# A feed-forward layer in groups of 256 tokens, with the last five groups' down projection as seven quarter products

## The chip, the cores and the metric

The kernel runs on one core of one Trainium2 chip. The metric is the device time of one execution in microseconds (us). Before the change three runs took 238.29, 239.14 and 239.62 us, with a median of 239.14.

The engines are TensorE (PE in the profile; its weight loads are PEld), VectorE (DVE), ScalarE (ACT), GpSimd (POOL) and SyncE (SP, which here only issues DMAs). Each engine works through its own instructions in order. SBUF is the on-chip memory, PSUM holds what TensorE writes.

## The reference, cut to what matters

```python
# attention: 4 batches, 8 heads, 768 positions, head dimension 64
scores = q @ k.T / 8 - slope[h] * dist        # kept: 8 global keys, 96 local keys
a = softmax(scores)
x = concat_heads(a @ v)                        # [4, 768, 512]
# token mixer of rank 32, then a feed-forward layer
u = x + (x.T @ U @ V).T
out = u + relu(u @ w_ch1) @ w_ch2              # w_ch1 512 x 2048, w_ch2 2048 x 512
```

The last line is what the change is about: an up projection (`u @ w_ch1`), a relu, a down projection (`@ w_ch2`) and the residual sum.

## The kernel before

**Attention.** The work goes pair by pair of heads: 4 batches x 4 pairs = 16 pairs, numbered i. The first four pairs (the first batch) run by themselves while the weights load. From then on, the loop over i (line 656) interleaves the attention of pair i with the mixer of pair i - 1 and with the feed-forward of earlier batches. One pass of the loop issues, for pair i, three blocks of scores (`st_S`, lines 333 and 340; VectorE adds the bias with L362, into `sp`), two exps on ACT (`st_E`, L374), and for pair i - 1 the products with v (`st_V`, lines 386 and 390, evacuated by VectorE at L395 and L409 and cast by POOL at L410) and the mixer: `st_M1` (L419, cast by VectorE at L423), `st_MT` (L436, cast at L437), `st_M3` twice (L473, added into x at L478), a POOL cast (L482) and a DMA transpose into `uT` (`st_X`, L462). The mixer's and the v products share one PSUM buffer, `ob`.

**Feed-forward before.** A batch's 768 tokens are two groups of 384. A group's up projection is 16 units, one for each 128 columns of w_ch1: four matmuls of 128x384 (L508) into a PSUM tile `hps` (three buffers of the tag `th`, shared with the transposes of q and k), then a relu on ACT into `htr` (L512). Its down projection is, for each of its three tiles of 128 tokens, four units of four matmuls of 128x512 (L528), accumulated in a PSUM tile `cps` (two buffers); after the fourth, VectorE adds x into `osb` (L534) and SP stores it. The very last tile is done as two halves of 16 matmuls of 128x256 (L546), each added and stored by itself (L551).

**What sets the order.** The order is written out by hand: between the pieces of attention stand calls `fill(n)`, each of which issues n units from two queues, `ups_q` and `downs_q`. `fill` mixes them four downs to three ups as far as both are there; a group's downs wait until all of its ups are issued, ups may run one group ahead, and no downs are issued before iteration 7 (`held`). A pass has 10 units in iterations 4 to 8 and 13 from 9 on. The groups of batch 0 are queued (`queue_ff`) before the loop, those of a later batch b when its last pair's mixer is done, in iteration 5 + 4b; what is left after iteration 17 is issued back to back.

**Weights.** w_ch1 comes as four DMAs of 512 columns each from POOL's queue (`load_w1`, L205), w_ch2 as four of 512 rows (`load_w2`, L208). Two ups are begun early (`begin_up`, L491), on the parts of `uT` that are ready.

Of the kernel before, what the change touches and what calls it, by code (L numbers as in the profile page):

```python
# [11 lines left out]
FP32 = mybir.dt.float32  # L12
FP16 = mybir.dt.float16
# [7 lines left out]
def kernel(  # L21
# [40 lines left out]
    NTG = GT // P  # L62

# [93 lines left out]
    reli = cst.tile([P, 256], I32, name="reli")  # L157
    nc.gpsimd.iota(reli, pattern=[[-1, 256]], base=0, channel_multiplier=1)
    ident = cst.tile([P, P], FP32, name="ident")
# [13 lines left out]
    relcat = cst.tile([P, 3, 256], FP32, name="relcat")  # L173
# [3 lines left out]
    def finish_table(t):  # L177
        nc.gpsimd.tensor_scalar_max(t[0:NG, 0, 0:P], relB[0:NG, 0:P], float(-NL))
        nc.gpsimd.memset(t[0:NG, :, P:], float(-NL))
# [8 lines left out]
    finish_table(rel16)  # L188
# [167 lines left out]
    relf = relcat.rearrange("p a c -> p (a c)")  # L356

    def s_dve(i, hi, got):
        sc, c0, tot, r0 = got
        if c0 == 0:  # L360
            sps[i, hi] = scp.tile([P, W], FP32, name=f"sp{hi}", tag=f"sp{hi}", bufs=1)
        nc.vector.scalar_tensor_tensor(  # L362
            out=sps[i, hi][:, c0:c0 + tot], in0=sc[:, 0:tot],
            scalar=qk_scale / slope[2 * (i % NP) + hi], in1=relf[:, r0:r0 + tot],
            op0=ALU.mult, op1=ALU.add,
        )
# [120 lines left out]
    def begin_up(jt, dcs, ps=None):  # L487
        if ps is not None:
            begun[jt] = [ps, 0]
        for dc in dcs:  # L490
            nc.tensor.matmul(  # L491
                begun[jt][0][:, 0:GT], w1_16[:, dc, jt * P:(jt + 1) * P], uTs[0][:, dc, 0:GT],
                start=(dc == 0), stop=False,
            )
        begun[jt][1] = dcs[-1] + 1

    def queue_ff(b, g):
        ts = slice(g * GT, (g + 1) * GT)
        uT, tmp16, x_sb = uTs[b], tmps[b], xs[b]
        cell = {}  # L500

        def mk_up(jt):
            def go():
                if jt == 0:
                    cell["htr"] = ffp.tile([P, NJC, GT], FP16, name="htr", tag="htr")
                hps, done = begun.pop(jt) if jt in begun else (ps_th("hps"), 0)
                for dc in range(done, NDC):
                    nc.tensor.matmul(  # L508
                        hps[:, 0:GT], w1_16[:, dc, jt * P:(jt + 1) * P], uT[:, dc, ts],
                        start=(dc == 0), stop=(dc == NDC - 1),  # L510
                    )
# [256 lines left out]
```

## Time and profile before

| | |
|---|---|
| median of three runs | 239.14 us |
| the profiled execution | 239.37 us, of which the span from first to last instruction is 237.6 |
| granted TensorE clock | 1.000 |
| HBM | 27.46 MB read, 6.29 MB written, 142 GB/s over the span |
| loads of q, k, v | 16 DMAs of 384 KB each, some 6 us to landing |
| loads of w_ch1 and w_ch2 | 8 DMAs of 512 KB, 10.8 us to landing |
| stores | 23 DMAs of 256 KB (2.3 us), 2 of 128 KB (1.7 us) |

In the lines that are shown below, a group of instructions has its line of kernel.py, the engine, the operation, the names written and read, the shapes and a count; then the busy time in us and the mean duration of one in ns; then the time that the engine stood idle just before them, and what ended it. A row of the timeline or of the chain has the start in us and the length in us; `x8` is eight instructions. A row of the stretches has the busy time of each engine with the count of its instructions. The strips of digits are the busy tenths in 40 slices of the span. Matmuls are pipelined, so the duration of one is longer than the spacing of a series.

### The profile page before, as it was taken

To read this page: it belongs to the slowest core of one execution; us is meant where nothing else is said; L and a number is where in the kernel's file an instruction comes from. 1 tells how busy PE (TensorE), PEld (TensorE's weight loads), DVE (VectorE), ACT (ScalarE), POOL (GpSimd) and SP (SyncE) were. 2 spreads that over 40 slices of the span, in tenths; PEclk is the share of its full clock that TensorE was granted. 3 is DMA by queue.
4 is the path that set the end of the run, shared out by engine and by line. 5 is a ranking of instruction groups with operands and counts; after the bars stand their busy time and mean duration, and the time that the engine had idled before them with its cause. 6 is when DMAs were issued, how large, how long until landed. Compare 5 with 4: busy or idle time off the path is not lost.

```text
span 237.6 us, 4921 instructions
## 1 busy us (share of the span) xinstructions
PE 226.9 (96%) x1964; PEld 126.3 (53%) x1964; DVE 124.8 (53%) x277; ACT 115.9 (49%) x200; POOL 79.7 (34%) x128
## 2 busy tenths in 40 slices
PE   7889959999999999999999999999999999999994
PEld 2446645656554445565555455565555555555553
DVE  3778857768686867574766675765433111011121
ACT  6767757886750403865544227474632244533200
POOL 7379937576361524242425151313111000000000
PEclk9999999999999999999999999999999999999999
DMA  6998999999989998896949581751212210011012
GB/s 197 294 287 239 261 241 229 259 229 175 223 177 227 222 233 197 214 194 157 241 127 234 168 231 36 205 25 39 75 50 46 77 47 30 14 44 47 14 75 88
DMA packets 86558, 36.61 MB, mean 154 GB/s; under 512 B 74152, under 2 KB 83592, under 8 KB 86536
## 3 DMA queue, kind: packets, MB, share of 16 engines
q1 hardware_dynamic: 81480, 32.01, 55.9%
q0 software_dynamic: 5056, 4.29, 11.3%
q8 instruction: 15, 0.25, 0.4%
q14 instruction: 7, 0.06, 0.1%
HBM read 27.46 MB, written 6.29 MB: 142 GB/s over the span
## 4 chain that ended last, share of the span: by engine, by line
PE 78%; DMA 7%; POOL 4%; ACT 4%; DVE 3%; issue 1%; SPq 1%; POOLq 0%
PE cps L528 34%; PE hps L508 31%; DMA w<-in_moe_w_ch_dram 4%; DMA kst<-in_k_dram 3%; PE sc L333 3%; ACT ep L374 2%; ACT htr L512 2%; PE ob L390 2%; PE cps L546 1%; PE ob L386 1%; PE sc L340 1%; POOL v L127 1%; PE sc L473 1%; POOL vA L272 1%; PE ob L419 1%
## 5 line engine op out<-in xcount | busy, mean ns | idle before, releaser
L512 ACT ACTIVATE htr<-hps 128x384 f16<-128x384 f32 x128 | 61.2, 492 | 84.1 <-PE hps L508 83.5
L508 PE MATMUL hps<-uT,w 128*128 128x384 f16 x506 | 97.6, 326 | 0.7 <-DVE uT L455 0.3
L528 PE MATMUL cps<-w,htr 128*128 128x512 f16 x368 | 91.3, 379 | 0.0
L508 PEld LDWEIGHTS <-w 128*128 128x128 f16 x506 | 45.5, 98 | 31.5 <-issue 0.7
L362 DVE SCALAR_TENSOR_TENSOR sp<-sc,relcat 128x512 f32<-128x512 f32 (+1 forms) x72 | 43.3, 641 | 23.7 <-PE sc L340 14.2
L528 PEld LDWEIGHTS <-htr 128*128 128x128 f16 x368 | 33.7, 98 | 32.2
L534 DVE TENSOR_TENSOR osb<-cps,x_sb 128x512 f32<-128x512 f32 x23 | 15.9, 690 | 49.7 <-PE cps L528 49.4
L374 ACT ACTIVATE ep<-sp 128x1408 f16<-128x1408 f32 x24 | 32.8, 1373 | 12.5 <-DVE sp L362 12.5
L410 POOL CAST x<-x_sb 128x384 f16<-128x384 f32 x30 | 15.4, 514 | 49.7 <-DVE x_sb L409 49.7
L482 POOL CAST x<-x_sb 128x768 f16<-128x768 f32 x12 | 10.0, 830 | 37.3 <-DVE x_sb L478 37.3
L333 PEld LDWEIGHTS <-kT 64*128 64x128 f16 x192 | 8.3, 93 | 16.9 <-issue 14.9
L409 DVE TENSOR_TENSOR x_sb<-ob,rcp 128x384 f32<-128x384 f32 x30 | 16.7, 557 | 1.0
L333 PE MATMUL sc<-qT,kT 64*128 64x128 f16 x192 | 16.7, 221 | 0.0
L390 PE MATMUL ob<-v,ep 128*128 128x65 f16 x192 | 16.0, 194 | 0.0
L390 PEld LDWEIGHTS <-ep 128*128 128x128 f16 x192 | 13.7, 98 | 3.0 <-issue 0.3
L340 PE MATMUL sc<-qT,kA 64*128 64x128 f16 x160 | 14.6, 217 | 0.7 <-DVE kA L264 0.3
L127 POOL CAST v<-vst 128x768 f16<-128x768 f32 x16 | 13.4, 840 | 4.0 <-DMA vst<-in_v_dram 4.0
L352 ACT ACTIVATE ep<-sc 128x512 f16<-128x512 f32 (+1 forms) x24 | 12.1, 559 | 5.3 <-PE sc L340 4.2
L386 PE MATMUL ob<-vA,ep 128*128 128x65 f16 x160 | 14.1, 194 | 0.2 <-DVE vA L285 0.2
L113 POOL CAST k<-kst 128x768 f16<-128x768 f32 x14 | 11.8, 845 | 1.4 <-ACT ep L352 1.0
L386 PEld LDWEIGHTS <-ep 128*128 128x128 f16 x160 | 11.0, 97 | 2.1
L113 POOL CAST q<-qst 128x768 f16<-128x768 f32 x13 | 10.9, 842 | 0.0
(85 smaller groups left out, 173.6 us busy)
## 6 DMA issues: line engine op xcount, KB each, us to landing
qst<-in_q_dram SPq DMA_DIRECT2D x16, 384.0 KB, 6.2
kst<-in_k_dram SPq DMA_DIRECT2D x16, 384.0 KB, 5.9
vst<-in_v_dram SPq DMA_DIRECT2D x16, 384.0 KB, 6.2
out_dram<-osb SPq DMA_DIRECT2D x23, 256.0 KB, 2.3
w<-in_moe_w_ch_dram POOLq DMA_DIRECT2D x8, 512.0 KB, 10.8
vA<-v SPq DMA_DIRECT2D x8, 152.3 KB, 3.5
out_dram<-osb SPq DMA_DIRECT2D x2, 128.0 KB, 1.7
uT<-x SPq DMA_TRANSPOSE x12, 4.5
```

Of the source, the lines that this page charges most:

```text
L113: turn_over(st16.rearrange("p n h d -> p h n d"), st)
L333: nc.tensor.matmul(scs[hi][:, o:o + P], kT[r, kb * P:(kb + 1) * P], qT[r, kb * P:(kb + 1) * P], start=(o == 0 and not on_pe), stop=(o + P ...
L340: nc.tensor.matmul(scs[hi][:, o + P:o + 2 * P], kA[r, kb], qT[r, (kb + 1) * P:(kb + 2) * P], start=False, stop=(o + 2 * P == tot),)
L362: nc.vector.scalar_tensor_tensor(out=sps[i, hi][:, c0:c0 + tot], in0=sc[:, 0:tot], scalar=qk_scale / slope[2 * (i % NP) + hi], in1=relf[:, ...
L374: nc.scalar.activation(ep, sps.pop((i, hi)), AF.Exp, scale=slope[2 * (i % NP) + hi])
L386: nc.tensor.matmul(ob[:, qi], ep[:, OF[qi - 1]:OF[qi - 1] + P], vA[:, qi - 1, hi], start=True, stop=False,)
L390: nc.tensor.matmul(ob[:, qi], ep[:, DG[qi]:DG[qi] + P], vt[:, qi, hi], start=(qi == 0), stop=True,)
L409: nc.vector.tensor_tensor(xo, ob[:, :, 0:D], rb, ALU.mult)
L508: nc.tensor.matmul(hps[:, 0:GT], w1_16[:, dc, jt * P:(jt + 1) * P], uT[:, dc, ts], start=(dc == 0), stop=(dc == NDC - 1),)
L512: nc.scalar.activation(cell["htr"][:, jt], hps[:, 0:GT], AF.Relu)
L528: nc.tensor.matmul(cps, htr[:, jc, t * P:(t + 1) * P], w2_16[:, jc], start=(b > 0 and jc == 0), stop=(jc == NJC - 1),)
L534: nc.vector.tensor_tensor(osb, cps, x_sb[:, n], ALU.add)
```

## The change

A batch becomes three groups of 256 tokens. An up unit now takes two column tiles of w_ch1 into the two halves of one `hps` tile: eight matmuls of 128x256 and one relu of 128x512; a group has eight such units. `htr` gets three buffers. `fill` alternates one down and one up, the passes have 8, 10 and 11 units, and ups may run one group ahead (two while downs are held). The results are added into x itself and stored from there; `osb` is gone.

The last five groups, `WG` (batch 2 groups 1 and 2, batch 3 groups 0 to 2), compute the down projection of a group, a product of 256 x 2048 by 2048 x 512, by quarters: with A cut into a11, a12, a21, a22 (two halves of tokens, two of the inner dimension) and B into b11 to b22, seven products of 128 x 1024 by 1024 x 256 (a Strassen scheme in Winograd's form) stand for eight. Each is a unit of eight matmuls of 128x256, and after each VectorE adds what the half bank holds by then into x. That needs sums of the quarters: of the weights once (t1 to t4; t3 is written over b12, the others into a tile with the tag of x_sb), and of each group's `htr` (s1 to s4). A sum is issued in two halves on VectorE, from a queue `jobs`: one after each unit, or at once where a product needs it. In a split group the ups are ordered so that the sums of the first half can be issued after four of the eight ups.

Beside that, three setup tiles move (`reli` and `ident` share a buffer of `ep0`, and `relcat` has 640 columns instead of 768, read by a broadcast in the second block of scores).

```diff
+    FT = 2 * P
+    NFG = S // FT
+    HJ = NJC // 2
+    HD = DM // 2
+    WG = ((2, 1), (2, 2), (3, 0), (3, 1), (3, 2))
...
+    def queue_sum(name, part, out_, a, b_, op):
+        def go():
+            nc.vector.tensor_tensor(out_, a, b_, op)
+            have.add((name, part))
+        jobs.append(go)
+
+    def need(*names):
+        while not all(n in have for n in names):
+            jobs.popleft()()
...
+        t = xp.tile([P, 3, HJ, HD], FP16, name="t16", tag="x_sb", bufs=3)
+        b11, b12, b21, b22 = quarters
+        tw.update(t1=t[:, 0], t2=t[:, 1], t3=b12, t4=t[:, 2])
+        for name, a, b_ in (("t1", b12, b11), ("t2", b22, tw["t1"]), ("t4", b21, tw["t2"])):
+            for k, js in enumerate((slice(0, HJ // 2), slice(HJ // 2, HJ))):
+                queue_sum(name, k, tw[name][:, js], a[:, js], b_[:, js], ALU.subtract)
...
+            for name, a, b_, op in (
+                ("s1", "a21", "a22", ALU.add), ("s2", "s1", "a11", ALU.subtract),
+                ("s4", "a12", "s2", ALU.subtract), ("s3", "a11", "a21", ALU.subtract),
+            ):
+                queue_sum((name, b, g), k, cell[name][:, js], cell[a][:, js], cell[b_][:, js], op)
...
-        def mk_up(jt):
+        def mk_up(at):
+            jp = at // 2 + (at % 2) * NJC // 4 if split else at
+
             def go():
...
-                hps, done = begun.pop(jt) if jt in begun else (ps_th("hps"), 0)
-                for dc in range(done, NDC):
-                    nc.tensor.matmul(
-                        hps[:, 0:GT], w1_16[:, dc, jt * P:(jt + 1) * P], uT[:, dc, ts],
-                        start=(dc == 0), stop=(dc == NDC - 1),
-                    )
-                nc.scalar.activation(cell["htr"][:, jt], hps[:, 0:GT], AF.Relu)
+                hps, done = begun.pop(jp) if jp in begun else (ps_th("hps"), 0)
+                for k in range(2):
+                    jt = 2 * jp + k
+                    for dc in range(done, NDC):
+                        nc.tensor.matmul(
+                            hps[:, k * FT:(k + 1) * FT],
+                            w1_16[:, dc, jt * P:(jt + 1) * P], uT[:, dc, ts],
+                            start=(dc == 0 and k == 0), stop=(dc == NDC - 1 and k == 1),
+                        )
+                nc.scalar.activation(
+                    cell["htr"][:, 2 * jp:2 * jp + 2].rearrange("p j t -> p (j t)"), hps, AF.Relu
+                )
+                if split and at % 4 == 3:
+                    queue_sums(at // 4)
             return go
...
-                    osb = ffp.tile([P, DM], FP32, name="osb", tag="osb", bufs=3)
-                    nc.vector.tensor_tensor(osb, cps, x_sb[:, n], ALU.add)
-                    nc.sync.dma_start(out[b, n * P:(n + 1) * P, :], osb)
+                    nc.vector.tensor_tensor(x_sb[:, n], cps, x_sb[:, n], ALU.add)
+                    store(n)
+                    if t == 1 and follow in WG:
+                        queue_last_weight_sum()
             return go
...
+        def mk_product(bank, half, a, w, dst, first=False, done=None):
             def go():
...
+                need(*(((a, b, g), k) for k in range(2) if a[0] == "s"))
+                need(*((w, k) for k in range(2) if w[0] == "t"))
+                ps = cell[bank][:, half]
+                for j in range(HJ):
+                    nc.tensor.matmul(
+                        ps, cell[a][:, j], tw[w][:, j], start=(first and j == 0),
+                        stop=(done is not None and j == HJ - 1), skip_group_check=True,
+                    )
+                n, cs = dst
+                nc.vector.tensor_tensor(x_sb[:, n, cs], ps, x_sb[:, n, cs], ALU.add)
+                for what in done or ():
+                    store(*what)
             return go
...
+            x1 = mk_product("cx", lo, "a11", "b11", (n0, lo), first=True)
+            x2 = mk_product("cx", lo, "s2", "t2", (n0, hi_))
+            x3 = mk_product("cx", lo, "s3", "t3", (n1, hi_), done=[(n1, hi_)] if last else None)
+            x4 = mk_product("cx", lo, "a22", "t4", (n1, lo), done=[(n1, lo)] if last else [(n1,)])
+            y1 = mk_product("cy", lo, "a12", "b21", (n0, lo), first=True)
+            y2 = mk_product("cy", hi_, "s1", "t1", (n1, hi_))
+            y3 = mk_product("cy", hi_, "s4", "b22", (n0, hi_), done=[(n0,)])
+            for made in (x1, y1, x2, y2, x3, y3, x4) if last else (x1, y1, y2, x2, y3, x3, x4):
+                downs_q.append((made, (b, g)))
...
     def fill(n):
         for _ in range(n):
...
+            unit()
+            if jobs:
+                jobs.popleft()()
+
+    def unit():
+        down = downs_q and not held[0] and not any(w == downs_q[0][1] for _, w in ups_q)
+        room = ups_q and (not downs_q or place(ups_q[0][1]) - place(downs_q[0][1])
+                          < (3 if held[0] else 2))
+        if down and (ahead[0] > 0 or not room):
+            ahead[0] = 0
+            downs_q.popleft()[0]()
+        elif room:
+            ahead[0] = 1
+            ups_q.popleft()[0]()
...
-        n = 1 if i < 2 * NP + 1 else 2
+        units = iter(
+            (1, 1, 1, 1, 1, 1, 1, 1, 0) if i + 1 < NPE
+            else (1, 1, 1, 2, 1, 1, 1, 1, 1) if i < 2 * NP + 1
+            else (2, 1, 1, 2, 1, 1, 1, 1, 1)
+        )
```

More of the change, by code (lines that the diff above doesn't have):

```diff
@@ L515, in mk_down @@
         def mk_down(t, part):
-            n = NTG * g + t
+            n = 2 * g + t
             def go():
+                if (t, part) == (0, 1) and not split and follow in WG:
+                    queue_weight_sums()
                 if part == 0:
@@ L696 @@
             break
-        more = 1 if i + 1 < NPE else 0
-        fill(n + more)
+        fill(next(units))
         if live:
@@ L712 @@
             st_E(i, 0)
-        fill(1)
+        fill(next(units))
         if i > NP:
@@ L728 @@
             turn(i + 2)
-        fill(n - more)
+        fill(next(units))
     while ups_q or downs_q:
```

150 lines of the change are left out of this document (78 added, 72 removed).

## The prediction

> **What bounds the kernel now.** I read the page's totals first, then the busy times by stretch, then the groups by shape, then the order of time on TensorE.
>
> ```profile
> span 237.6 us, 4921 instructions
> PE 226.9 (96%) x1964; PEld 126.3 (53%) x1964; DVE 124.8 (53%) x277; ACT 115.9 (49%) x200; POOL 79.7 (34%) x128
> PE   7889959999999999999999999999999999999994
> DVE  3778857768686867574766675765433111011121
> PE 78%; DMA 7%; POOL 4%; ACT 4%; DVE 3%; issue 1%; SPq 1%; POOLq 0%
> ```
>
> ```profile
> 40.00:50.00 10.00, 9.33 (x102) 5.64 (x100) 6.91 (x13) 8.00 (x15) 7.29 (x12) 1.00 1.19 250
> 50.00:140.00 90.00, 89.87 (x829) 49.31 (x826) 61.55 (x136) 42.27 (x64) 35.74 (x52) 1.00 0.94 200
> 150.00:160.00 10.00, 9.87 (x100) 6.11 (x97) 6.37 (x15) 7.16 (x13) 1.76 (x3) 1.00 0.69 116
> ```
>
> The columns of the stretches are length, then busy PE, weight loads, DVE, ACT, POOL, the granted clock (1.00 throughout) and DMA. From 50 us on TensorE has hardly an idle moment: what shortens its instruction stream there shortens the kernel, and what makes it wait lengthens it. Before 50 us it waits for other things, and a change there is worth what it does to those waits. VectorE has 36% to spare beside attention and almost everything after 172 us.
>
> **What the feed-forward costs on TensorE, before and after.**
>
> ```profile
> L508 PE MATMUL hps<-uT,w 128*128 128x384 f16 x506 | 97.6, 326 | 0.7 <-DVE uT L455 0.3
> L491 PE MATMUL hps<-uT,w 128*128 128x384 f16 x6 | 1.3, 328 | 2.0 <-DMA w<-in_moe_w_ch_dram 2.0
> L528 PE MATMUL cps<-w,htr 128*128 128x512 f16 x368 | 91.3, 379 | 0.0
> L546 PE MATMUL cps<-w,htr 128*128 128x256 f16 x32 | 3.7, 273 | 0.0
> L546 PEld LDWEIGHTS <-htr 128*128 128x128 f16 x32 | 3.1, 98 | 0.6
> ```
>
> ```profile
> 181.48 4.32 PE cps L528 x20
> 199.85 3.90 PE hps L508 x24
> ```
>
> ```profile
> 230.61 3.66 PE L546 MATMUL cps<-w,htr 128*128 128x256 f16 x32
> ```
>
> A duration (326, 379 ns) contains the way through the array; the spacing is what counts. The pieces of the chain give 4.32/20 = 216 ns for 512 columns and 3.90/24 = 162.5 ns for 384. The timeline's row for 256 columns gives (3.66 - 0.273)/31 = 109.3 ns, with a weight load of 98 ns still hidden under it. So the fixed part of a step is 2 to 3 ns, and a step costs by its columns.
>
> - Up projection: 506 + 6 = 512 steps x 162.5 ns = 83.2 us become 4 x 3 x 64 = 768 steps of 256 columns x 109.3 ns = 83.9 us: **+0.7 us**.
> - Down projection: 368 x 216 ns + 32 x 109.3 ns = 83.0 us become 224 x 216 ns (seven plain groups) + 5 x 7 x 8 = 280 steps x 109.3 ns (the split groups) = 79.0 us: **-4.0 us**. Each split group needs 56 x 109.3 ns = 6.1 us where 32 x 216 ns = 6.9 us stood.
>
> Together **-3.3 us**, all of it on the engine that sets the end. Everything below is subtracted from that.
>
> The Trainium skill ("TensorE: Matmul & The Clock Gate", section Back-to-back issue gap) gives a sustained spacing of about 81 ns at 128 columns and 131 ns at 512, by which narrow steps would be poor value. Here the spacings are 109.3 and 216 ns; by the Trainium skill, interpolated as an estimate, a product step would take 98 ns, a split group 5.5 us against 4.2 us, and the change would lose. The trace disagrees with these spacings of the Trainium skill.
>
> **The first ups, 34 to 50 us.** The built order of the changed kernel has the eight units of the first group in loop iteration 4, each unit taking two column tiles of w_ch1; so units 3, 5 and 7 are the first that need quarters 1, 2 and 3 of w_ch1. Before, iteration 4 issued ten units of one tile each, tiles 0 to 9, and quarter 3 was first needed behind the transposes at 43.95 us.
>
> ```profile
> L205 POOL DMA_DIRECT2D w<-in_moe_w_ch_dram x2: 742/746/750, 27.5 to 28.2; - x2
> DMA to landing us min/median/max: 11.6/12.9/14.2
> ```
>
> ```profile
> 34.11 0.48 PE L508 MATMUL hps<-uT,w 128*128 128x384 f16 x2 [0.32 <-DVE uT L455]
> 35.39 0.81 PE L508 MATMUL hps<-uT,w 128*128 128x384 f16 x4
> 36.54 2.12 PE L508 MATMUL hps<-uT,w 128*128 128x384 f16 x12
> 38.87 2.77 PE L508 MATMUL hps<-uT,w 128*128 128x384 f16 x16
> 41.58 0.23 PE L333 MATMUL sc<-qT,kT 64*128 64x128 f16 x2
> 43.95 0.49 PE L233 MATMUL tp<-ident,q 128*128 128x128 f16 x6 [0.23 <-ACT htr L512]
> ```
>
> ```profile
> 34.90 1.27 DVE L362 SCALAR_TENSOR_TENSOR sp<-sc,relcat 128x512 f32<-128x512 f32 x2
> ```
>
> ```profile
> PE ob L419 <- POOL x L410: 0.4, 1, 0.4
> ```
>
> Quarter 2 lands at 27.5 + 11.6 = 39.1 us, quarter 3 at 28.2 + 14.2 = 42.4 us (the minimum is the first load's); the change leaves these loads and what stands ahead of them on POOL alone. The working for the new order: the second block of scores still ends at 36.5 us, because it waits for the two adds that VectorE ends at 36.17. Units 3 and 4 take 2 x 0.87 us, to 38.3; the third block of scores to 38.7; then a wait of 0.45 us for quarter 2; units 5 and 6 to 40.9; a wait of 1.6 us for quarter 3; units 7 and 8 to 44.25. The scores of iteration 5 then start at 44.3 instead of 41.58, 2.7 us later. In that time 16 x 256 instead of 10 x 384 columns have been issued, two thirds of an old unit or 0.45 us more work: a loss of 2.2 us. Two waits of iteration 5 shrink as the other engines catch up meanwhile (the 0.23 us at 43.95 and the 0.4 us of L419 for POOL): 0.55 us back. **+1.65 us**. From 50 us on TensorE has no slack in which to make it up. The bounds are 1.0 (more is given back, or the loads land earlier) and 2.7 (nothing is).
>
> **The half sums, about 145 to 172 us.** The sums of the split groups are new VectorE work: eight of 128x1024 f16 for the weights, then eight of 128x512 f16 in each of five groups, and 35 adds of 128x256 in place of 10 of 128x512. For groups 2 to 5 of these (after 172 us) VectorE is a tenth busy, so they are hidden; what counts is the stretch in which the weight sums and the first group's sums meet the last two attention pairs. No row shows an f16 add with both inputs in SBUF. The nearest:
>
> ```profile
> L362 DVE SCALAR_TENSOR_TENSOR sp<-sc,relcat 128x512 f32<-128x512 f32 x48 | 31.1, 685 | 17.3 <-PE sc L340 14.2 <-ACT htr L512 2.3 <-ACT ep L374 0.8
> L534 DVE TENSOR_TENSOR osb<-cps,x_sb 128x512 f32<-128x512 f32 x23 | 15.9, 690 | 49.7 <-PE cps L528 49.4
> L551 DVE TENSOR_TENSOR osb<-cps,x_sb 128x256 f32<-128x256 f32 x2 | 0.8, 424 | 2.4 <-PE cps L546 2.4
> L308 DVE COPY kA<-kT 128x640 f16<-128x640 f16 x8 | 2.5, 316 | 0.0
> ```
>
> At one element a cycle a sum of 512 costs 690 ns and one of 1024 costs 690 + 512 x 266/256 = 1222 ns; at two, 424 and 690 ns. The f16 copy (640 elements in 316 ns) shows that f16 can go faster than one, so I take 424 and 690 ns; even the copy's rate would give no less than about 290 and 415 ns. Eight of each is 8.9 us. They are popped one per unit over some 17 us, in which VectorE has 3.6 us in 10 free, 6.2 us, and some 2 us more because queued operations overlap: two adds of 685 ns took 1.27 us above, 0.1 us less than their sum, and there are over twenty operations. That just about fits. Where it doesn't, the engine's queue is in order, so behind a sum stand the casts between the transposes of the mixer (M1, MT, M3), each with one unit of 0.87 us to spare on TensorE, and the single `ob` buffer. One such place can be read off the new order: the first sum of the second split group is issued in the same unit as the up whose relu it needs, so it holds VectorE until 0.8 us after that up; with its own 0.42 us, the cast behind it ends about 0.45 us after TensorE wants it.
>
> Beside a POOL cast this can be worse, as these two rows show, where a copy that takes 0.28 us by itself takes 0.96:
>
> ```profile
> 22.27 0.96 DVE L285 COPY vA<-v 8x520 f16<-8x520 f16 x1
> 27.49 0.28 DVE L285 COPY vA<-v 8x520 f16<-8x520 f16 x1
> ```
>
> ```profile
> 22.25 0.84 POOL L113 CAST q<-qst 128x768 f16<-128x768 f32 x1
> ```
>
> The Trainium skill ("SBUF — State Buffer", section Who interferes with whom) states for a VectorE operation with two SBUF inputs that it and a GpSimd operation that reads SBUF lock each other out. The trace has no such operation, only the copy above, which agrees in kind.
>
> Bounds for this stretch: 0 (all fits) and +4 (the sums at one element a cycle add 6.4 us more to a full VectorE, of which the later group's slack returns a third). I take **+0.8 us**, nearer to nothing since the two-element price is nearer to the f16 row: 0.45 for the place named and the rest for collisions with POOL.
>
> **The rest.** The last group's products alternate between two PSUM banks, so an add (0.42 us, and 273 - 109 ns for the last columns' way through the array) has 0.87 us; with sums queued ahead of it the first repeat is some 0.15 us late: **+0.15 us**. The end is unchanged in shape, a 256-wide add and a 128 KB store after the last matmul. Relus:
>
> ```profile
> L512 ACT ACTIVATE htr<-hps 128x384 f16<-128x384 f32 x128 | 61.2, 492 | 84.1 <-PE hps L508 83.5
> L352 ACT ACTIVATE ep<-sc 128x512 f16<-128x512 f32 x16 | 8.7, 594 | 4.3 <-PE sc L340 4.2
> ```
>
> ```profile
> 95.32 0.86 ACT htr L512 x2
> 96.18 1.27 ACT ep L374
> 97.88 1.46 PE hps L508 x8
> ```
>
> 96 x 0.594 = 57 us replace 61.2 us, so ACT is no bound. Three hps buffers now cover 2.6 us of TensorE instead of 1.95, more than an exp (1.37 us) and a relu; the chain passes through ACT at 95 to 97 us and the ups behind it take 1.46 instead of 1.30 us. Two such places should go: **-0.3 us**. Storing x_sb itself instead of osb changes no wait, since nothing writes these rows again; t16 reuses the buffer of batch 1, whose last store is issued some eight units before the first weight sum.
>
> **The sum.** -3.3 + 1.65 + 0.8 + 0.15 - 0.3 = -1.0 us. The profiled execution took 239.37 us (span 237.6 and 1.8 around it), 0.2 more than the median of the three runs, 239.14; the forecast for a run is 239.14 - 1.0 = **238.1 us**, with a range of its own of 236.9 to 239.3.
>
> **Rivals.**
> 1. *VectorE falls behind* in the stretch of the weight sums: at more than about 0.55 us for a 512-wide sum the work no longer fits, and the mixer's casts, then the scores' buffers, hold TensorE. The stretch costs 3.3 us instead of 0.8: 240.6 us, slower. For it: 64% busy before, in-order queue, POOL rows above. Against it: f16 copies at half the time per element.
> 2. *The early wait is given back or smaller, and the sums fit*: 1.0 instead of 1.65 and 0.1 instead of 0.8, and the removed waits are 0.6: 236.4 us. For it: queued VectorE operations overlap. Against it: quarter 3 lands at 42.4 us whatever TensorE does.
> 3. *Seven products don't run as seven*: each waits for the add before it on its half bank, 0.27 us at 15 places, 4 us, and the saving is gone: 242 us. Against it: an up stands between two products in four of the five groups.
> 4. *Narrow steps gain little*: if halving the columns took off a quarter and not half, a step of 256 would cost 0.75 x 216 = 162 ns, and the 280 product steps 14.8 us more: 253 us. The row of the 32 steps speaks against it. The spacings of the Trainium skill above would have this sign.
>
> **How the numbers follow.** 0.5% of 239.14 is 1.2 us, about what a measurement of this kernel can tell from no change. The forecast has 0.50 (0.20 of it beyond -1.2 us, 0.30 within), rival 2 has 0.24, rival 1 has 0.22, rival 3 has 0.03, rival 4 has 0.01. Faster by over 0.5%: 0.20 + 0.24 = 0.44; within: 0.30; slower: 0.26. The range goes from rival 2 with every uncertain cost at its low end (235.9) to rival 1 with the stretch at +4 (241.3).
>
> **What would show it.** On TensorE in the changed kernel: steps of 128x256 spaced 109 ns; two waits for w_ch1 near 39 and 41 to 42.4 us, 2.0 us together; no waits of ups for ACT in the dense stretches; in the stretch of the last two pairs, waits for VectorE casts of under 1 us in all, and f16 sums of 0.42 and 0.69 us. Wrong would be: sums of 0.7 and 1.2 us, w_ch1 landing before 41 us, or waits between a group's products.

## The result and the profile after

The changed kernel takes **236.8 us** (median of 8 runs, 236.26 to 237.52), the kernel before 239.47 on the same chip (8 runs, 238.18 to 240.74): a ratio of **0.9893, 95% interval 0.9861 to 0.9926**, which is 2.6 us less (1.8 to 3.3). Unedited copies gave 0.9906 [0.9871, 0.9940] for the changed kernel and 1.0001 [0.9976, 1.0026] for the kernel before. The forecast was 238.1 us: the sign and the full range (235.9 to 241.3) held, but the result lies just below the forecast's own range (236.9 to 239.3), and 1.0 us less had been expected where 2.6 came. The profiled execution took 236.67 us.

The totals of the changed kernel's page, with the strips of TensorE and VectorE:

```profile
span 234.8 us, 5675 instructions
PE 224.0 (95%) x2324; PEld 161.4 (69%) x2324; DVE 151.4 (65%) x349; ACT 112.2 (48%) x169; POOL 80.3 (34%) x128
PE   7989977999999999999999999999999999999994
DVE  3677866468686777566667576779896543454452
```

VectorE went from 124.8 to 151.4 us busy, and its strip shows where: a hill of 9, 8 and 9 in the slices from 158 to 176 us, which the strip of before did not have. The same kernel by stretches (length, then busy PE, weight loads, DVE, ACT, POOL, the granted clock, DMA):

```profile
40.00:50.00 10.00, 8.57 (x111) 6.99 (x111) 5.45 (x11) 7.04 (x10) 5.46 (x9) 1.00 1.20 252
50.00:140.00 90.00, 89.68 (x916) 58.19 (x915) 61.22 (x135) 41.87 (x53) 36.05 (x54) 1.00 0.90 195
160.00:165.00 5.00, 5.00 (x63) 3.37 (x60) 4.97 (x10) 1.52 (x3) 1.91 (x3) 1.00 0.35 92
170.00:175.00 5.00, 5.00 (x58) 4.46 (x56) 4.97 (x10) 2.52 (x5) 0.83 (x1) 1.00 0.17 58
```

TensorE lost time at 40 to 50 us (8.57 of 10 where before had 9.33), and nothing to speak of later, although VectorE is busy 4.97 us in 5 in two stretches. The groups by shape:

```profile
L582 PE MATMUL hps<-uT,w 128*128 128x256 f16 x756 | 96.4, 273 | 2.1 <-DMA w<-in_moe_w_ch_dram 1.7 <-DVE uT L464 0.3
L519 DVE TENSOR_TENSOR s<-htr 128x512 f16<-128x512 f16 x20 | 9.3, 463 | 12.7 <-ACT htr L587 12.7
L632 PE MATMUL cx<-t,s 128*128 128x256 f16 x40 | 5.2, 273 | 0.0
L519 DVE TENSOR_TENSOR s<-htr,s 128x512 f16<-128x512 f16 x10 | 4.2, 420 | 0.2
L519 DVE TENSOR_TENSOR t<-w,t 128x1024 f16<-128x1024 f16 x4 | 2.6, 682 | 0.0
```

Products (L632) wait for nothing, ups (L582) wait 1.7 us for w_ch1, and the f16 sums take 420 and 682 ns (424 and 690 were assumed), except two, of 0.98 and 0.72 us, that stretch the mean of the row `s<-htr` to 463. Their cause is looked for below.

**One number apart from the medians.** The first up can start when the first quarter of w_ch1 has landed, and that moment turned out to vary from execution to execution. These are TensorE's first early up in the timeline of before, and in that of the changed kernel, and, of the changed kernel, the first product of the mixer (L428) for the last time but two, and the last product of all (start, length):

```profile
31.65 0.50 PE L491 MATMUL hps<-uT,w 128*128 128x384 f16 x2 [2.01 <-DMA w<-in_moe_w_ch_dram]
```

```profile
30.43 0.61 PE L502 MATMUL hps<-uT,w 128*128 128x256 f16 x4 [0.78 <-DMA w<-in_moe_w_ch_dram]
...
155.76 0.30 PE L428 MATMUL ob<-u,x 128*128 128x32 f16 x6
...
230.44 1.04 PE L632 MATMUL cx<-t,htr 128*128 128x256 f16 x8
```

From the start of the first up to the end of the last matmul is 234.27 - 31.65 = 202.62 us before (the last row of before, 230.61 + 3.66, stands in the prediction) and 231.48 - 30.43 = 201.05 us after: **1.57 us less**. This stretch hardly depends on when the quarter landed: two executions of the reordered kernel below, whose first ups start 2.03 us apart, agree in it to 0.01 us. So it tells a part of the change to some tenths, where a median of six runs tells 0.8 us. But loads that land later than the first quarter can still add to it: the 0.23 us between the two executions of the changed kernel are nearly all the wait for quarter 2.

A still shorter stretch is sharper: from the L428 row above (155.76 us in the changed kernel, just ahead of its first weight sum; L419 in the kernel before) to the end of the last matmul. Executions of one kernel agree in it to 0.02 us. It can be compared only between kernels that issue the same work ahead of that row, so among the rows of before, or among the others, and not across. The table has both stretches for every kernel; the ratio is to the kernel before on the same chip. A run that is over 1.5% longer than the fastest of its kernel is left out of the ratio, which concerns one run of before and one of the weight sums twice (245.30 us, the profiled one).

| kernel | median us (runs) | ratio, 95% interval | first up at | first up to last matmul | L428 to last matmul |
|---|---|---|---|---|---|
| before, first profile | 239.14 (3) | | 31.65 | 202.62 | 80.93 |
| before, copy | 239.17 (12) | 1.0001 [0.9976, 1.0026] | 31.57 | 202.60 | 80.93 |
| before, setup tiles moved | 238.66 (12) | 1.0008 [0.9983, 1.0034] | 30.93 | 203.06 | 80.93 |
| changed | 236.80 (8) | 0.9893 [0.9861, 0.9926] | 30.43 | 201.05 | 75.72 |
| changed, copy | 236.18 (6) | 0.9906 [0.9871, 0.9940] | 29.83 | 200.82 | 75.70 |
| groups of 256 alone | 240.42 (7) | 1.0067 [1.0043, 1.0092] | 30.92 | 204.10 | 79.02 |
| sums left out | 235.98 (6) | 0.9875 [0.9839, 0.9910] | 30.55 | 200.50 | 75.05 |
| first ups reordered | 236.09 (6) | 0.9887 [0.9839, 0.9934] | 31.51 | 199.51 | 75.71 |
| the same again | 235.09 (6) | 0.9856 [0.9815, 0.9897] | 29.48 | 199.50 | 75.70 |
| sums ahead of the unit | 236.58 (11) | 0.9915 [0.9885, 0.9945] | 30.55 | 200.92 | 75.87 |
| reordered and sums ahead | 236.17 (6) | 0.9892 [0.9856, 0.9927] | 31.64 | 199.68 | 75.87 |
| weight sums twice | 243.58 (6) | 1.0185 [1.0144, 1.0227] | 32.91 | 207.31 | 81.95 |
| all sums twice | 250.34 (6) | 1.0497 [1.0466, 1.0528] | 30.67 | 214.40 | 89.41 |
| weight sums on GpSimd | 240.33 (10) | 1.0087 [1.0053, 1.0121] | 28.89 | 206.32 | 80.57 |

Two executions of one kernel agree in the first of the two stretches to 0.23 us or better, while their first up starts up to 2 us apart. Between kernels it can differ by more without a cause in the edit: with the setup tiles moved it is 0.44 us longer, all of it one wait for a GpSimd cast at 68.6 us, and the second stretch is the same.

### The profile page after: what moved, and what is told of

The parts are those of the page before. It is cut to its first block, busy times and chain, and to the rows that moved or that the text cites. A ratio compares the mean times of both kernels' runs of the same rounds, so it can differ in the third digit from the quotient of the medians.

```text
span 234.8 us, 5675 instructions
## 1 busy us (share of the span) xinstructions
PE 224.0 (95%) x2324; PEld 161.4 (69%) x2324; DVE 151.4 (65%) x349; ACT 112.2 (48%) x169; POOL 80.3 (34%) x128
## 4 chain that ended last, share of the span: by engine, by line
PE 77%; POOL 7%; DMA 7%; DVE 3%; ACT 1%; issue 1%; SPq 0%; POOLq 0%
PE hps L582 32%; PE cps L612 21%; PE cx L632 7%; DMA w<-in_moe_w_ch_dram 6%; PE cy L632 5%; PE sc L339 3%; PE ob L399 2%; DMA kst<-in_k_dram 2%; PE ob L395 1%; POOL v L132 1%; POOL x L419 1%; PE sc L346 1%; POOL vA L278 1%; PE tp L239 1%; POOL k L118 1%
## 5 line engine op out<-in xcount | busy, mean ns | idle before, releaser
L587 ACT ACTIVATE htr<-hps 128x512 f16<-128x512 f32 x96 | 56.9, 597 | 87.2 <-PE hps L582 84.4
L582 PE MATMUL hps<-uT,w 128*128 128x256 f16 x756 | 96.4, 273 | 2.1 <-DMA w<-in_moe_w_ch_dram 1.7
L582 PEld LDWEIGHTS <-w 128*128 128x128 f16 x756 | 70.3, 98 | 13.2 <-DMA w<-in_moe_w_ch_dram 2.2
L612 PE MATMUL cps<-w,htr 128*128 128x512 f16 x224 | 56.9, 379 | 0.0
L612 PEld LDWEIGHTS <-htr 128*128 128x128 f16 x224 | 19.1, 97 | 16.6
L419 POOL CAST x<-x_sb 128x384 f16<-128x384 f32 x30 | 15.8, 526 | 42.2 <-DVE x_sb L418 38.8
L519 DVE TENSOR_TENSOR s<-htr 128x512 f16<-128x512 f16 x20 | 9.3, 463 | 12.7 <-ACT htr L587 12.7
L418 DVE TENSOR_TENSOR x_sb<-ob,rcp 128x384 f32<-128x384 f32 x30 | 16.7, 557 | 1.0
L632 PEld LDWEIGHTS <-s 128*128 128x128 f16 x160 | 15.5, 98 | 1.9
L399 PEld LDWEIGHTS <-ep 128*128 128x128 f16 x192 | 13.7, 98 | 2.6 <-DVE x_sb L418 0.3
L637 DVE TENSOR_TENSOR x_sb<-cx,x_sb 128x256 f32<-128x256 f32 x20 | 8.5, 423 | 10.1 <-PE cx L632 10.0
L632 PEld LDWEIGHTS <-htr 128*128 128x128 f16 x120 | 11.7, 98 | 1.3
```

Source lines behind the costliest of these rows:

```text
L399: nc.tensor.matmul(ob[:, qi], ep[:, DG[qi]:DG[qi] + P], vt[:, qi, hi], start=(qi == 0), stop=True,)
L418: nc.vector.tensor_tensor(xo, ob[:, :, 0:D], rb, ALU.mult)
L419: nc.gpsimd.tensor_copy(x16, xo)
L582: nc.tensor.matmul(hps[:, k * FT:(k + 1) * FT], w1_16[:, dc, jt * P:(jt + 1) * P], uT[:, dc, ts], start=(dc == 0 and k == 0), stop=(dc == ...
L587: nc.scalar.activation(cell["htr"][:, 2 * jp:2 * jp + 2].rearrange("p j t -> p (j t)"), hps, AF.Relu)
L612: nc.tensor.matmul(cps, htr[:, jc, t * P:(t + 1) * P], w2_16[:, jc], start=(b > 0 and jc == 0), stop=(jc == NJC - 1),)
```

## The experiments

**Theory A** is the prediction's sum: the seven products save 4 us, the rest of the change gives some 2.5 of it back, in the first ups (waits for w_ch1) and in VectorE's queue. Against it stood a VectorE that falls behind (rival 1), waits that are given back later (rival 2), and, after the result, the setup tiles as the source of an earlier landing (theory C).

**Groups of 256 alone.** `wg_none` keeps the new groups and has no split group.

```diff
-    WG = ((2, 1), (2, 2), (3, 0), (3, 1), (3, 2))
+    WG = ()
```

> The changed kernel with no split group: groups of 256 tokens alone, every down projection by 16 matmuls of 512 columns. Theory A (the change gained 2.6 us as the sum of -4.0 for the product steps, +0.7 for the narrower up steps, about 2.1 for the waits for w_ch1, 0.6 for VectorE, and the rest by earlier landings): without the split the product steps' 4.0 come back and VectorE's 0.6 go, so 3.4 us slower than the changed kernel, 240.2 us, a ratio to before of 1.003. Theory B (the gain comes from the regrouping, the split is hidden or eaten by its sums): within 1 us of the changed kernel, ratio under 0.994.

Measured: 240.42 us, 1.0067 [1.0043, 1.0092], 1.5 us longer than before from the first up on. Its 384 full-width down steps are back:

```profile
L612 PE MATMUL cps<-w,htr 128*128 128x512 f16 x384 | 96.8, 379 | 0.0
```

So the regrouping alone is a loss, as the sum had it (0.7 + 1.65 - 0.3 = 2.05 us, measured 1.5), and the split must win: 204.10 - 201.05 = 3.05 us with its sums and its stalls, or, in the sharper stretch, 79.02 - 75.72 = 3.30.

**The half sums left out.** `no_sums` issues none of them; the products read plain quarters, so the outputs of the five split groups are not computed. The number of products and adds stays.

```diff
-                queue_sum((name, b, g), k, cell[name][:, js], cell[a][:, js], cell[b_][:, js], op)
+                cell[name] = cell[{"s1": "a21", "s2": "a11", "s4": "a12", "s3": "a11"}[name]]
...
-        tw.update(t1=t[:, 0], t2=t[:, 1], t3=b12, t4=t[:, 2])
...
+        tw.update(t1=b11, t2=b22, t3=b12, t4=b21)
...
```

> The changed kernel without the half sums: the 56 sums on VectorE are left out and each product reads a quarter in place of a sum (this part of the result is not computed). Theory A (the sums fit beside the rest but for two waits of 0.39 and 0.17 us): 0.6 us faster than the changed kernel, 236.2 us, ratio 0.987. Theory B (VectorE is the hidden price of the split): 2 us or more faster, ratio under 0.981.

Measured: 235.98 us, 0.9875 [0.9839, 0.9910]. From the first up on it is 0.55 us shorter than the changed kernel (0.32 shorter than its copy), from L428 on 75.72 - 75.05 = 0.67. VectorE in the stretch that was full:

```profile
160.00:165.00 5.00, 5.00 (x63) 3.37 (x62) 3.73 (x7) 1.30 (x4) 2.11 (x3) 1.00 0.35 92
```

All the sums together cost TensorE some 0.65 us. Against the groups of 256 alone the seven products then save 79.02 - 75.05 = **3.97 us**. (The longer stretch gives 3.6, but there the two executions also differ by waits for the loads and by one at 102 us, ahead of any product.)

**Where that half microsecond is.** The only idle time that the timeline of the changed kernel marks on TensorE from 155 to 182 us is at the place that the prediction named: the first sum of the second split group, in VectorE's queue ahead of the mixer's cast L432. TensorE's rows (the last), then VectorE's:

```profile
174.84 1.03 PE L632 MATMUL cy<-t,s 128*128 128x256 f16 x8
175.88 0.20 PE L399 MATMUL ob<-v,ep 128*128 128x65 f16 x1
...
179.00 1.03 PE L632 MATMUL cy<-w,s 128*128 128x256 f16 x8
180.26 0.23 PE L445 MATMUL ob<-ident,zw 128*128 128x128 f16 x1 [0.23 <-DVE zw L432]
```

```profile
179.67 0.43 DVE L519 TENSOR_TENSOR s<-htr 128x512 f16<-128x512 f16 x1 [1.08 <-ACT htr L587]
180.02 0.18 DVE L432 CAST zw<-ob 128x32 f16<-128x32 f32 x1
```

The sum waits for its relu, the cast waits behind the sum, and the product waits for the cast. By the spacing of starts TensorE loses 180.26 - 179.00 - 8 x 0.1093 = 0.39 us here (the idle time in the row is shorter, because the matmul before is counted busy until its last column is through the array). The same reckoning finds a second place, which the timeline doesn't mark: 175.88 - 174.84 - 8 x 0.1093 = 0.17 us, where the products with v wait for the evacuation L418, behind sums in VectorE's queue. `sum_ahead` issues the sum a little later, so that the cast goes first:

```diff
         for _ in range(n):
-            unit()
             if jobs:
                 jobs.popleft()()
+            unit()
```

> One line moved: a half sum is issued ahead of the unit instead of behind it, so the first sum of the second split group no longer stands ahead of the mixer's cast (L432) on VectorE. Theory A (the place named in the prediction is an order on VectorE's queue, worth 0.4 us): the TensorE wait of 0.39 us at the MT product disappears, nothing as large comes in its place, 0.2 to 0.5 us less than the changed kernel (about 236.2), too little to be told by the medians, but the trace shows it. Rival (VectorE is full there, so the wait only moves to the next cast): the sum of the waits after 155 us stays at 0.5 to 0.6 us.

Measured: 236.58 us, 0.9915 [0.9885, 0.9945], and 200.92 us from the first up on, between the two of the unedited kernel; from L428 on it takes 75.87 us, 0.15 more than that. The waits at 176 and 180 us are gone, and there is another one, an iteration earlier (TensorE, then VectorE):

```profile
169.44 0.23 PE L445 MATMUL ob<-ident,zw 128*128 128x128 f16 x1 [0.44 <-DVE zw L432]
```

```profile
168.87 0.41 DVE L519 TENSOR_TENSOR s<-htr 128x512 f16<-128x512 f16 x1
169.21 0.18 DVE L432 CAST zw<-ob 128x32 f16<-128x32 f32 x1
```

The expected gain didn't come: the rival holds. A sum of the first group, issued later than before, now stands ahead of the previous cast. With VectorE's queue this full, the new order only chose another one to wait.

**How near the edge is VectorE?** `w_sums_twice` issues t1, t2 and t4 twice, 6 x 0.68 = 4.1 us more; `sums_twice` does so with every sum but t3 (`1 if name == "t3" else 2`).

```diff
-            nc.vector.tensor_tensor(out_, a, b_, op)
+            for _ in range(2 if name in ("t1", "t2", "t4") else 1):
+                nc.vector.tensor_tensor(out_, a, b_, op)
```

> Only the weight sums t1, t2 and t4 are issued twice: 6 x 0.68 = 4.1 us more on VectorE, at 156 to 170 us. In the changed kernel VectorE is 4.97 us in 5 busy at 160 to 165 us, and idle for 0.9 us at 169 to 170. Theory F (VectorE is full there, and what is added is passed on but for that idle time): the end is 2.5 to 4.1 us later, 239 to 240.6. Rival (being busy all the time still leaves slack, since its queue runs behind with nobody waiting): under 1 us.

> Every half sum is issued twice (t3, which is written over its own input, once), so VectorE gets 6 more of 128x1024 (4.1 us) and 40 more of 128x512 (16.8 us). Theory A (the sums fit, the cost is one cast queued behind a sum): the first split group has little slack left, 6 us of sums more in a stretch that had about 2 us free; 1 to 3 us longer than the changed kernel, 238 to 240. Rival (VectorE has far more slack than I counted): under 0.7 us longer.

Measured: 243.58 us, 1.0185 [1.0144, 1.0227], and 250.34 us, 1.0497 [1.0466, 1.0528]. Both expectations were too low. From the first up on, 4.1 us of added sums cost 207.31 - 201.05 = 6.3 us, from L428 on 81.95 - 75.72 = 6.2. The profiled run of `w_sums_twice` is the longest of its six; `sums_twice` has the same three waits with the same lengths. TensorE of `w_sums_twice`, and VectorE's row in the longest of the waits:

```profile
167.01 0.21 PE L339 MATMUL sc<-qT,kT 64*128 64x128 f16 x1 [0.80 <-DVE sp L371]
167.61 0.21 PE L339 MATMUL sc<-qT,kT 64*128 64x128 f16 x1 [0.39 <-DVE sp L371]
...
171.65 0.19 PE L399 MATMUL ob<-v,ep 128*128 128x65 f16 x1 [2.68 <-DVE x_sb L418]
```

```profile
168.08 2.73 DVE L520 TENSOR_TENSOR t<-w,t 128x1024 f16<-128x1024 f16 x4
```

Four sums in a row hold the attention's evacuation (L418), and with it the one `ob` buffer, for 2.7 us; and behind the wait TensorE also runs at a lower clock, of which more below. By the end of that wait 4.7 of the 6.2 us are lost, and the other 1.5 by 176.5 us, where the clock is back. The changed kernel sits at the edge: what it has costs it some 0.65 us, the next 4 us would cost all they take and half as much again.

**The weight sums on GpSimd.** `w_sums_pool` gives t1, t2 and t4 to an engine that is a fifth busy there.

```diff
-            nc.vector.tensor_tensor(out_, a, b_, op)
+            eng = nc.gpsimd if name in ("t1", "t2", "t4") else nc.vector
+            eng.tensor_tensor(out_, a, b_, op)
```

> The weight sums t1, t2 and t4 go to GpSimd, which is a fifth busy there, instead of VectorE. If a two-input operation on VectorE and one on GpSimd hold each other up (as the sums of 0.72 and 0.98 us instead of 0.41 beside a GpSimd cast suggest), the adds of VectorE that run beside them become longer and the casts of GpSimd for the mixer come later: slower than the changed kernel by 1 to 5 us. Rival (the long sums have another cause, GpSimd is free help): VectorE drops below full at 160 to 165 us and the time is within 0.5 us of the changed kernel.

Measured: 240.33 us, 1.0087 [1.0053, 1.0121], 5.3 us longer than the changed kernel from the first up on and 4.85 from L428 on, as expected. Rows of GpSimd, VectorE and TensorE of this kernel:

```profile
154.19 4.29 POOL L520 TENSOR_TENSOR t<-w 128x1024 f16<-128x1024 f16 x2 [0.97 <-DMA out_dram<-x_sb]
...
161.30 6.65 POOL L520 TENSOR_TENSOR t<-w,t 128x1024 f16<-128x1024 f16 x3
...
169.52 0.50 POOL L419 CAST x<-x_sb 128x384 f16<-128x384 f32 x1
```

```profile
156.53 1.98 DVE L315 COPY kA<-kT 128x32 f16<-128x32 f16 x1
162.33 1.38 DVE L520 TENSOR_TENSOR s<-htr 128x512 f16<-128x512 f16 x1
```

```profile
170.08 0.32 PE L428 MATMUL ob<-u,x 128*128 128x32 f16 x6 [3.01 <-POOL x L419]
```

On GpSimd a weight sum takes 2.1 us instead of 0.68. VectorE's own operations beside it are held up (a sum 1.38 us instead of 0.41, a copy of 0.17 us 1.98), and the casts for the mixer queue behind it on GpSimd, until TensorE waits 3 us. The same contention, in small, fits the two long sums of the changed kernel. Here are GpSimd's rows and VectorE's:

```profile
172.89 0.83 POOL L491 CAST x<-x_sb 128x768 f16<-128x768 f32 x1 [5.45 <-DVE x_sb L487]
175.88 0.64 POOL L419 CAST x<-x_sb 128x384 f16<-128x384 f32 x1 [2.16 <-DVE x_sb L418]
```

```profile
173.01 0.98 DVE L519 TENSOR_TENSOR s<-htr 128x512 f16<-128x512 f16 x1
...
175.74 0.41 DVE L519 TENSOR_TENSOR s<-htr 128x512 f16<-128x512 f16 x1
```

The first sum starts 0.12 us after the cast and ends 0.27 us after it, as if it had waited for nearly the whole cast. The second starts ahead of its cast and takes its usual 0.41 us; here the cast is longer, 0.64 us instead of 0.51. The Trainium skill ("SBUF — State Buffer", section Who interferes with whom) says that a VectorE operation with two SBUF inputs and a GpSimd operation that reads SBUF exclude each other, the first one holding the other until it is done; these rows agree, now with the two-input operation that the trace of before did not have.

**The first ups.** `ups_w1` issues the units of quarters 0 and 1 of w_ch1 for the first two groups, then those of quarters 2 and 3 for both, so that the later quarters are needed eight units later.

```diff
...
+                for half in range(2):
+                    for gg in range(2):
+                        for at in range(4 * half, 4 * half + 4):
+                            ups_q.append((mks[gg](at), (b, gg)))
...
```

> The changed kernel with the ups of batch 0 in another order: the first four units of groups 0 and 1 (quarters 0 and 1 of w_ch1) ahead of the last four of both. Theory A (the two idle times of TensorE at 38 and 40 us, 2.1 us together, are the price of asking for quarters 2 and 3 early, and nothing later makes them up): both waits are gone and the kernel is 1.5 to 2.1 us faster than the changed one, about 235.0 us, ratio 0.981. Theory B (TensorE would have waited there for VectorE and ACT anyway, or catches up later): under 0.6 us faster, ratio 0.987 or above.

> The reordered first ups again (units of w_ch1 quarters 0 and 1 of two groups first), now on the same chip as the copy of the changed kernel. If the two waits for w_ch1 cost what my sum says (1.65 us, bounds 1.0 to 2.7), it takes 1.0 to 2.0 us less than the copy: ratio to the copy 0.992 to 0.996. Rival: TensorE would have stood still for other things anyway in iteration 5, then it is within 0.5 us of the copy. It must not depend on the landing: with both waits gone, the last matmul starts at about 230 us or earlier if the first quarter lands as early as in the first profile of the changed kernel.

Measured: 236.09 us, 0.9887 [0.9839, 0.9934]; again, beside the copy of the changed kernel, 235.09 us, 0.9856 [0.9815, 0.9897]. The first ratio by itself would have been read for theory B (0.987 or above). The changed kernel's TensorE, with its two waits, and the landing of its quarters 2 and 3 (issued at 27.5 and 28.2 us, as before); below them TensorE in the second execution of the reordered one:

```profile
34.76 0.21 PE L339 MATMUL sc<-qT,kT 64*128 64x128 f16 x1 [0.26 <-DVE sp L371]
35.35 0.21 PE L339 MATMUL sc<-qT,kT 64*128 64x128 f16 x1 [0.39 <-DVE sp L371]
...
35.67 1.92 PE L582 MATMUL hps<-uT,w 128*128 128x256 f16 x16
...
38.17 1.92 PE L582 MATMUL hps<-uT,w 128*128 128x256 f16 x16 [0.31 <-DMA w<-in_moe_w_ch_dram]
41.52 1.92 PE L582 MATMUL hps<-uT,w 128*128 128x256 f16 x16 [1.43 <-DMA w<-in_moe_w_ch_dram]
43.37 0.23 PE L339 MATMUL sc<-qT,kT 64*128 64x128 f16 x2
```

```profile
DMA to landing us min/median/max: 10.6/11.9/13.2
```

```profile
36.84 3.67 PE L583 MATMUL hps<-uT,w 128*128 128x256 f16 x32
40.44 0.23 PE L339 MATMUL sc<-qT,kT 64*128 64x128 f16 x2
```

Both waits are gone, and from the first up on the two executions take 199.51 and 199.50 us against 201.05 and 200.82: **1.3 to 1.5 us**, as the wait was priced. From L428 on they agree with the changed kernel to 0.02 us, so all of it is won early and none is lost later. In the medians the two kernels can't be told apart: 235.09 against 236.18 us on the same chip, with intervals that overlap.

**Both edits.** `both` has the reordered ups and the sums ahead of the unit.

> The reordered first ups and the half sums ahead of the unit together. If the two losses that the sum named beside the saving (1.65 and 0.8 us) are what keeps the change from its 3.3 us, most of it is back: about 1.4 + 0.3 us less than the changed kernel, 234.7 (234.2 to 235.6), ratio to the kernel before 0.982 to 0.986. If VectorE's queue holds it anyway, no better than the reordered ups alone (235.1).

Measured: 236.17 us, 0.9892 [0.9856, 0.9927], 199.68 us from the first up on and 75.87 from L428 on. The expectation of 234.7 was missed; as the second alternative has it, moving the sums adds nothing to the reordered ups (it costs 0.16 us). Its first quarter landed late, 31.64 us. A version that is better than the changed kernel by 1.3 to 1.5 us, the reordered ups alone, is thus in the traces, and not in the medians.

**The setup tiles, and two copies.** `before_again` and `after_again` are unedited. `before_setup` is the kernel before with the three setup tiles of the change:

```diff
-    reli = cst.tile([P, 256], I32, name="reli")
+    setup = scp.tile([P, 384], I32, name="setup", tag="ep0")
+    reli = setup[:, 0:256]
...
-    relcat = cst.tile([P, 3, 256], FP32, name="relcat")
+    relcat = cst.tile([P, 640], FP32, name="relcat")
...
```

> The kernel before with nothing but the three setup tiles moved as in the change (reli and ident in a buffer of ep0, relcat of 640 columns). Theory C (the setup tiles make the early stretch faster): first quarter of w_ch1 at 30.4 to 30.9 us and 238.0 us or less, ratio 0.995. Theory A (they do nothing): 239 us, ratio 0.998 to 1.002, landing like that of the kernel before in other executions.

> A copy of the changed kernel, unedited, beside its own reordering on the same chip. Question: did the w_ch1 quarters land about 1 us earlier than in the kernel before (30.4 against 31.6 us for the first) because of this execution, or because of the change? Theory A (chance of the execution, or of the chip): the first quarter lands anywhere between 30.4 and 31.6 us, and the profiled time moves with it by up to 1 us. Theory C (the change does it, through its setup tiles): it lands at 30.4 to 30.9 again. Time by both 236.0 to 237.5, ratio 0.986 to 0.993.

Measured: 238.66 us, 1.0008 [0.9983, 1.0034], so the setup tiles are worth nothing, although in its profiled execution the first up started at 30.93 us. Theory C falls. Over the table the first up starts anywhere between 28.89 and 32.91 us, and both ends are kernels whose order up to there is that of the changed kernel. For `before_again` another landing than 31.6 us was expected if it is chance, and 31.6 again, within 0.2, if the change brings the loads forward: it was 31.57. The copy of the changed kernel gave 29.83 us, earlier than either of its theories allowed. Chance is the likelier reading, since kernels of one order differ by up to 4 us, but it is not shown: the three profiles of kernels with the old groups average 31.4 us, the eleven others 30.7.

## Why the prediction came out as it did

Its sum from the first up on was -1.0 us; measured is -1.6 (-1.8 in the copies). The traces can be divided into the same terms. A step takes 2.6 ns and 0.417 ns for each column (from the spacings of 216 and 109.3 ns), and what lies between the starts of two matmuls beyond that is lost. The places over 0.13 us, from the first up on (good to some 0.2 us in a sum, by what lies under 0.13):

| lost on TensorE, us | before | changed | difference | predicted |
|---|---|---|---|---|
| first ups, to 51 us | 1.76 | 3.93 | +2.2 | +1.65 |
| ups that wait for relus, at 97.5 and 157.4 us | 0.58 | 0 | -0.6 | -0.3 |
| mixer, at 60 and 167 us before, at 109 changed | 0.58 | 0.21 | -0.4 | none |
| half sums, at 176 and 180 us | 0 | 0.55 | +0.55 | +0.95 |
| together | 2.92 | 4.69 | +1.8 | +2.3 |

What is left of the -1.6, -1.57 - 1.77 = -3.3 us, is the shorter instruction stream, as predicted. So the mechanism held, and that the sum of the losses came within 0.5 us is in part luck: its errors have opposite signs. Term by term:

- **Spacings of narrow steps: right.** Steps of 256 columns run at 109 ns in ups and products alike (the reordered ups above: (3.67 - 0.273)/31 = 109.6 ns). Predicted -4.0 for the downs; measured 3.97 us between the groups of 256 alone and the sums left out. Rival 4 falls, and with it, for this kernel, the spacings of the Trainium skill ("TensorE: Matmul & The Clock Gate", section Back-to-back issue gap) that the prediction held against its own.
- **The early waits: place and size right, the loss around them too small.** Predicted 0.45 and 1.6 us; the rows show idle times of 0.31 and 1.43, and between starts the second is 41.52 - 38.17 - 16 x 0.1093 = 1.60 us. Quarter 3 took 13.2 us from issue to landing (14.2 assumed), and the early up began earlier by about as much. Iteration 5 gives back 0.56 us, as assumed (0.55). What the sum left out are the units that are begun early: they are now 12 matmuls of 256 columns instead of 6 of 384, 0.34 us more, ahead of everything that leads to the second block of scores. So that block doesn't "still" end where it did: the ups behind it start 35.67 - 30.43 = 5.24 us after the first up, where before had 36.54 - 31.65 = 4.89, and the scores of iteration 5 start 3.0 us later instead of 2.7. The reordered ups take away the waits for w_ch1 alone, and of those 1.3 to 1.5 us stay won.
- **The half sums: the right place, a bit less.** 0.8 + 0.15 predicted, some 0.65 measured. The 0.45 us for the cast behind the first sum of the second split group was 0.39. Collisions with GpSimd happen as described (0.98 us for 0.41), and can have cost no more than the 0.17 us at 176 us, where the evacuation that TensorE waits for stands behind the long sum; the last group's banks cost nothing.
- **The waits for relus: two places, as named, but misread and too small.** The prediction set 1.46 us for the ups at 97.88 us against 8 x 0.1625 = 1.30, but 1.46 is what eight steps take with no wait, 7 x 0.1625 + 0.326. The loss stands ahead of that row: the scores before it start at 97.53 us, and 97.88 - 97.53 less a step of 0.06 is 0.29 us. The other place, at 157.4 us, has 0.29 too. Both are gone (the third row is the changed kernel's, right behind a matmul at 97.40).

```profile
97.53 0.22 PE L340 MATMUL sc<-qT,kA 64*128 64x128 f16 x2
97.88 1.46 PE L508 MATMUL hps<-uT,w 128*128 128x384 f16 x8
...
97.57 1.04 PE L582 MATMUL hps<-uT,w 128*128 128x256 f16 x8
```

- **The bounds of the stretch: wrong.** The prediction put at most +4 us on it, with a third of an overload returned later. Adding 4.1 us to VectorE costs 6.2, with nothing returned. Rival 1 didn't come true, but its price of 3.3 us was too low for the load at which it starts, and the forecast stood nearer to that edge than 0.8 us of cost makes it look: VectorE is 4.97 us in 5 busy for two stretches.
- **The step that failed for the time itself: "Quarter 2 lands at 39.1 us, quarter 3 at 42.4".** The landing of one execution was taken as fixed. The whole chain hangs on it from the first quarter on, so it moves the end by as much, and the wait for quarter 3 keeps its size (1.40 to 1.49 us idle wherever the order of the ups is the changed kernel's and the clock is full), since the ups move along with the loads. In the changed kernel's profile the first up started 1.2 us earlier than in that of before, and the medians differ by 2.6 us where the stretch behind it differs by 1.6. The copy has 2.2 (1.4 to 3.1) and 1.8. The rest is within the scatter of the runs, and what sets the landing stays open. Both profiles issue the load at 21.0 us, so it is the load itself that takes 10.6 us in one and 9.4 in the other. Rival 2's time of 236.4 was met, but not by its mechanism: its early wait of 1.0 and its sums of 0.1 are both lower than what was found.

## What to carry to other kernels

A chain that starts at a landing is best compared from that landing on: two profiles then tell tenths of a microsecond, and behind the last load that is waited for, hundredths, where medians of six runs tell 0.8. In this kernel a stretch in which a helper engine is almost full cost little as long as hardly anybody waited for it, and then more than all that was added; so look for the nines in its strip before giving it more. Shifting one operation didn't help there. Where a tile of weights is loaded in parts, the order of its first uses can be worth nearly as much as what a change of the arithmetic leaves after its costs: here 1.3 to 1.5 us against 1.6.

## What the runs showed of the hardware

The granted clock of TensorE, 1.00 throughout in the changed kernel, fell after waits of 2.7 us and more: 2.68 (both kernels with sums twice), 2.80 (the wait for the first quarter of w_ch1 in `w_sums_twice`) and 3.01 us. A wait of 2.47 us for that quarter, in the copy of the kernel before, left it at 1.00. In `w_sums_pool`, behind the wait of 3.01 us, the stretches and the next down steps read:

```profile
165.00:170.00 5.00, 2.07 (x18) 0.97 (x16) 4.77 (x7) 1.16 (x2) 5.00 (x5) 1.00 0.00 0
170.00:175.00 5.00, 4.92 (x34) 3.33 (x35) 2.38 (x6) 2.73 (x4) 0.03 (x1) 0.66 0.21 61
```

```profile
171.17 1.90 PE L613 MATMUL cps<-w,htr 128*128 128x512 f16 x4
```

Four steps take 1.90 us that take 1.04 elsewhere in this kernel, and the mean of 0.66 over 5 us is, as an estimate, 5 x 0.34 = 1.7 us lost beside the wait itself. The Trainium skill ("TensorE: Matmul & The Clock Gate", Part 1) puts the fall to half rate after an idle window of about 3.4 us; the trace agrees in kind, but here shorter waits, of 2.68 to 3.01 us, were enough. That is most of why the weight sums twice lose more than the work that was added (1.5 of the 2.1 us beyond it): a long wait is paid twice.
